# Four subtractions of a key minimum on GpSimd in place of VectorE, in a linear-attention block on one core

## The chip, the cores and the metric

The kernel runs on one core of one Trainium2 chip. The metric is the device time of one execution in microseconds (us). The core has five engines that run their own lists of instructions in order and wait for one another through semaphores: TensorE (PE, matrix products), VectorE (DVE), ScalarE (ACT), GpSimd (POOL) and SyncE (SP, which issues the DMAs here).

## What is computed

One transformer block with adaptive layer norm, a linear attention whose feature map is a pair of softmaxes, and a ReLU network. Batch 1, 2048 rows, width 576, 32 heads of 18, inner width 4608, all bf16.

```python
mod = (silu(c) @ w_mod).reshape(1, 6, 1, 576)          # sa, ca, ga, sb, cb, gb
h = layernorm(x) * (1 + ca) + sa
q, k, v = heads(h @ wqkv)                              # 32 heads of 18
pq, pk = q @ w_phi[head], k @ w_phi[head]
phi_q = concat([softmax(pq), softmax(-pq)])            # 36 features
phi_k = concat([softmax(pk), softmax(-pk)])
kv = sum_s phi_k[s, f] * v[s, d];  z = sum_s phi_k[s, f]
o = (phi_q @ kv) / (phi_q @ z + 1e-6)
x = x + ga * (o @ wo)
h = layernorm(x) * (1 + cb) + sb
x = x + gb * (relu(h @ w1) @ w2)
```

Both softmaxes are made stable by a shift: the first exponentiates pk - max(pk), the second min(pk) - pk, where maximum and minimum run over the 18 features of a head.

## The kernel before

The 2048 rows are 16 tiles of 128 rows. Keys are kept in four blocks of four tiles (`phik`), queries in blocks of two tiles (`room`). A tile has 11 groups of three heads; a group has 108 columns, of which the first 54 hold the key features from the projection, and later the first softmax, and the last 54 the second.

For a pair of key tiles p (p from 0 to 7, two pairs to a block) the softmax goes through these steps, which have short names in the kernel's list:

- KE: ACT copies the projected keys from PSUM into the first 54 columns (helper at L92).
- MN and MX, once for a block: a tree of minima or maxima on DVE (L457, L459, L460), whose last step (L462) writes a `root`. Roots take turns in four buffers.
- LO.p: minimum less key, from the first 54 columns into the last 54 (L470), one instruction over 128 partitions x 1188 elements.
- HI.p: key less maximum, in place in the first 54 columns (L472). It overwrites what LO.p reads, so it comes behind it.
- EX.p: one exponential on ACT over both halves, 2376 elements (L499).
- SU.p and SA.p: the sums, on PE into PSUM (L506) and on DVE (L510), or for two pairs on DVE alone with SD (L517).
- RC.p: the reciprocal, on ACT (L522, L524).
- SC.p: the scaling by it, on DVE (L530).

The queries have the same steps, with a q ahead of the name (qMN, qMX, qLO, qHI, qSA, qSC); their scaling is L534, and they aren't touched by the change. The steps J are the projections on PE (L574, L580), VE and QE copy values and queries out of PSUM on ACT (L92), MH modulates the normalized rows on ACT (L409) or DVE (L410), RW makes the gate rows on PE (L387).

When all keys of a range of tiles are scaled, KVa (tiles 0 to 11), KVb (12 and 13) and KVc (14 and 15) multiply keys and values on PE (L644), 11 products to a tile. KVE copies the result out, NU multiplies it with the first queries (L685), and the network of the first rows follows. A loop over the other seven blocks of 256 rows comes after it, in which PE does the network (L834, L826, L877) while the other engines prepare the next block.

The order of the work in the first stage is written out by hand: a list of step names, run through by a loop that calls each step. The order on PE, DVE, ACT and SP is that of the calls; POOL, too, runs its instructions in the order in which they are issued. Waits are put in by the framework from the tiles that a step reads and writes. Pair p's steps are in block p // 2, at tile p % 2 * 2. A number behind a step's name can choose the engine through the tuple `VA`.

POOL does memsets alone: constants, zero columns of `wk_raw`, `wo_sb`, `phik` and `room` (L203 to L207, L549, L550, L606, L621), and the identity.

Of the kernel before, what the change touches and what calls it, by code (L numbers as in the profile page):

```python
# [13 lines left out]
ALU = mybir.AluOpType  # L14
# [35 lines left out]
def kernel(  # L50
# [23 lines left out]
    V, A_, G, T_ = nc.vector, nc.scalar, nc.gpsimd, nc.tensor  # L74
# [372 lines left out]
    def softmax_parts(E, src, n, whole):  # L447

        ng = n * NG

        def slots(a, s=0):
            return a[:, :, :, s * GF:(s + 1) * GF].rearrange("p n g (f c) -> p (n g) f c", c=G2)

        def ext(op):
            src_, w = src.rearrange("p n g c -> p (n g) c"), 4 * G2
            a = work.tile([P, 4 * NG, w], BF16, name="tree", tag="tree", bufs=1)[:, 0:ng]
            V.tensor_tensor(out=a, in0=src_[:, :, 0:w], in1=src_[:, :, w:2 * w], op=op)  # L457
            for w in (2 * G2, G2):
                V.tensor_tensor(out=a[:, :, 0:w], in0=a[:, :, 0:w], in1=a[:, :, w:2 * w], op=op)  # L459
            V.tensor_tensor(out=a[:, :, 0:G2], in0=a[:, :, 0:G2], in1=src_[:, :, 8 * G2:9 * G2], op=op)  # L460
            r = work.tile([P, 4 * NG, 2, GH], BF16, name="root", tag="root", bufs=4)[:, 0:ng]
            V.tensor_tensor(out=r, in0=a[:, :, 0:GH].unsqueeze(2).to_broadcast([P, ng, 2, GH]),  # L462
                            in1=a[:, :, GH:G2].unsqueeze(2).to_broadcast([P, ng, 2, GH]), op=op)
            return r.rearrange("p a e h -> p a (e h)")

        def less(j, mn, mx):
            f = slots(src[:, j:j + 2])
            r = (mn if mx is None else mx)[:, j * NG:(j + 2) * NG].unsqueeze(2).to_broadcast([P, 2 * NG, DH // 2, G2])
            if mx is None:
                V.tensor_tensor(out=slots(E[:, j:j + 2], 1), in0=r, in1=f, op=ALU.subtract)  # L470
            else:
                V.tensor_tensor(out=slots(E[:, j:j + 2], 0), in0=f, in1=r, op=ALU.subtract)  # L472

        t = {}

        def low_root():
            t["mn"] = ext(ALU.min)

        def low_less(j):
            less(j, t["mn"], None)  # L480

        def high_root():
            t["mx"] = ext(ALU.max)

        def high_less(j):
            less(j, None, t["mx"])

        def low():
            low_root()
            for j in range(0, n, 2):  # L490
                low_less(j)

        def high():
            high_root()
            for j in range(0, n, 2):
                high_less(j)

        def exps(j, k=1):
            A_.activation(out=E[:, j:j + k], in_=E[:, j:j + k], func=ACT.Exp)  # L499

        def sums_pe(j):

            ps = t["s", j] = aux_tile("ps_sum")[:, 0:2 * NG * 2 * G2].rearrange("p (a c) -> p a c", c=G2)
            e = E[:, j:j + 2].rearrange("p n g (s c) -> p (n g) s c", s=2)
            for f in range(DH // 2):
                T_.matmul(ps, lhsT=ident[:], rhs=e[:, :, :, f * G2:(f + 1) * G2], start=(f == 0), stop=(f == DH // 2 - 1))  # L506

        def sums_add(j):
            l = t["l", j] = work.tile([P, 4 * NG, GH], FP32, name="ln_s", tag="ln_s", bufs=2)
            V.tensor_reduce(out=l[:], in_=t["s", j].rearrange("p a (e h) -> p a h e", h=GH), op=ALU.add,  # L510
                            axis=mybir.AxisListType.X)

        def sums(j):
            b, k = j // 2 * 2, j % 2
            if ("l", b) not in t:
                t["l", b] = work.tile([P, 4 * NG, GH], FP32, name="ln_s", tag="ln_s", bufs=2)
            V.tensor_reduce(out=t["l", b][:, k * 22:(k + 1) * 22].rearrange("p (g s) h -> p g s h", s=2), op=ALU.add,  # L517
                            axis=mybir.AxisListType.X, in_=E[:, j].rearrange("p g (s f h) -> p g s h f", s=2, h=GH))

        def recip(j):  # L520
            l = t["l", j]
            A_.activation(out=l[:], in_=l[:], func=ACT.Ln)  # L522
            r = t["r", j] = work.tile([P, 4 * NG, 2, GH], BF16, name="rsum", tag="rsum", bufs=3)
            A_.activation(out=r[:], in_=l[:].unsqueeze(2).to_broadcast([P, 4 * NG, 2, GH]), func=ACT.Exp, scale=-1.0)  # L524

        def scale(j):
            r = t["r", j][:].rearrange("p a e h -> p a (e h)")
            if whole:
                e = E[:, j:j + 2].rearrange("p n g (s f c) -> p (n g s) f c", s=2, c=G2)
                V.tensor_tensor(out=e, in0=e, in1=r.unsqueeze(2).to_broadcast([P, 4 * NG, DH // 2, G2]), op=ALU.mult)  # L530
                return
            for s in range(2):
                e, q = slots(E[:, j:j + 2], s), r.rearrange("p (a s) c -> p a s c", s=2)[:, :, s]
                V.tensor_tensor(out=e, in0=e, in1=q.unsqueeze(2).to_broadcast([P, 2 * NG, DH // 2, G2]), op=ALU.mult)  # L534

        class parts:
            pass
        for f in (low_root, low_less, high_root, high_less, low, high, exps, sums_pe, sums_add, sums, recip, scale):
            setattr(parts, f.__name__, staticmethod(f))
        return parts  # L540
# [214 lines left out]
    soft = {}  # L755
# [36 lines left out]
    p1_ctx = ExitStack()  # L792
    w1 = {}
    ln2 = norm_stats(0, U, xn1[0])
    VA = (V, A_)

    def kvs(t0, t1):
        return lambda: kv_part(t0, t1)
# [92 lines left out]
    def y(n, j, cols=HALVES):  # L891
# [6 lines left out]
    steps = {  # L898
        "RS": lambda u: ln[u][2](), "LX": lambda t, a=0: ln[t // U][4](t % U, VA[a]), "LS": lambda t: ln[t // U][1](t % U), "LT": ln1_T,
        "PT": ln1_pe, "PX": lambda u, c, a=0: ln1_out(u, c, VA[a]), "MH": lambda b, c, a=0: ln1_mod(b, c, VA[a]),  # L900
        "SIL": silu, "WBD": feature_maps, "CR": lambda: V.tensor_copy(out=crep[:], in_=siluc[:].to_broadcast([P, KC, 32])),
        "WT": fold_T, "WTE": lambda g, a=0: fold_T_out(g, VA[a]),
        "F1": lambda c: fold(1, c), "FA1": lambda c, a=0: fold_out(1, c, 0, VA[a]),
        "FB1": lambda c, a=0: fold_out(1, c, 1, VA[a]),
# [5 lines left out]
        "OPEN": open_p1, "PM": pad_keys, "LH": load_maps, "SD": lambda t: soft["K", t // TPB].sums(t % TPB),  # L910
        "J": project, "KE": keys_out, "VE": values_out, "QE": queries_out,
        "MN": lambda b: soft["K", b].low_root(), "MX": lambda b: soft["K", b].high_root(),
        "LO": lambda p: soft["K", p // 2].low_less(p % 2 * 2), "HI": lambda p: soft["K", p // 2].high_less(p % 2 * 2),
        "EX": lambda p: soft["K", p // 2].exps(p % 2 * 2, 2), "SU": lambda p: soft["K", p // 2].sums_pe(p % 2 * 2),
        "SA": lambda p: soft["K", p // 2].sums_add(p % 2 * 2),
        "RC": lambda p: soft["K", p // 2].recip(p % 2 * 2), "SC": lambda p: soft["K", p // 2].scale(p % 2 * 2),
# [27 lines left out]
    MN.0 RS.7 FB0.4 F0.1 KE.7 LT.9 F0.2 LT.11 FA0.4.1 FA0.1.1 FA0.2.1 LT.8 F0.0 FA0.0.1 FB0.1 FB0.0.1 F0.3 FB0.2  # L944
    LS.13 FA0.3.1 J.4.5 RS.6 LO.0 LX.12 KE.4 FB0.3.1 J.34.35 LX.14.1 LX.15 KE.5 LX.13 LT.10 MX.0 MH.2.3.1
    MH.2.0.1 MH.2.1 LM.1 MN.1 QE.2 QE.3 MH.2.4.1 MH.2.2.1 J.32.33 QE.0 LO.1 HI.0 QE.1 J.10.11 KE.10 EX.0 KE.11
    HI.1 LT.15 LT.14 MC2.0 LT.12 LO.3 J.8.9 MX.1 KE.8 LT.13 J.26.27 MH.3.2.1 MH.3.3.1 MH.3.4 LO.2 qMN.0 HI.2
    KE.9 VE.10 MH.3.0.1 LM.2 MH.3.1.1 LM.0 MC2.1 MC2.3 MC2.4 VE.11 MN.2 MC2.2 RW RWE.1 qMX.0 qHI.0 HI.3 MCE2
    EX.2 J.12.13 KE.12 KE.13 LO.4 J.14.15 KE.14 SD.0 SD.1 J.20.21 EX.3 MX.2 KE.15 SU.3 SA.3 EX.1 VE.4 RC.0 VE.5
    SU.2 RD.2 qLO.0 J.22.23 VE.6 qEX.1 qEX.0 J.30.31 SA.2 HI.4 RC.3 VE.14 VE.15 VE.7 LO.5 HI.5 qSU.0 RD.1 MX.3  # L950
    MN.3 qSA.0 EX.4 SU.1 RC.2 J.24.25 VE.8 SU.4 W1 SC.0 J.28.29 qRC.0 LW.0.0 RD.0 VE.9 EX.5 VE.12 SC.2 SA.1 LO.7
    SA.4 SC.3 VE.13 RC.1 J.40.41 QE.8 SU.5 RC.4 J.44.45 HI.7 LO.6 LW.1.1 HI.6 qSC.0 SA.5 EX.6 QE.9 SC.1 QE.12
    J.42.43 EX.7 SC.4 RC.5 QE.13 QE.10 SD.12 SD.13 SC.5 SU.7 SA.7 RC.6 RC.7 KVa SC.6 WOL KVb SC.7 KVc QE.11 WS.1
    qT.0 KVE.1.1 KVE.0 NU.0 NUE.0 NU.1 J.38.39 QE.6 OT.0 OTE.0 NUE.1 OT.1 OTE.1 WS.0 qMX.1 qHI.1 QE.7 WO.0 WOE.0
    WO.1 WOE.1 LW.2.1 J.36.37 QE.4 J.46.47 S2.0 S2.1 R2 QE.14 X2 PN QE.5 PNE P2 qMN.1 LW.0.1 LW.3.0 LW.1.0 QE.15
    LW.3.1 LW.2.0 G.0 FW.2 FW.1 qLO.1 RL.0 qEX.2 qEX.3 qMN.2 qLO.2 qSD.2 RL.2 RL.1 W2.2.0 G.1 qSD.3 W2.1.0 qRC.1
    FW.4 RL.3 W2.0.0 FW.5 W2.0.1 W2.1.1 qMX.2 qHI.2 RL.4 qSC.1 qT.1 W2.2.1 qEX.5 RL.5 G.2 FW.8 RL.6 NV.0 NVE.0
    OU.0 FW.7 NV.1 Y.1.0.0 Y.1.0.1 NVE.1 qEX.4 RL.8 RL.7 Y.1.0.2 OU.1 qSD.4 qSD.5 WP.0 YE.1.0 Y.0.0.0 WPE.0
    qRC.2 qSC.2 S3.0 WP.1 qT.2 WPE.1 Y.0.0.1 Y.0.0.2 S3.1 R3 Y.0.1.0 YE.0.0 Y.1.1.0 Y.0.1.1 X3 XT Y.0.1.2 MD.1
    MD.2 MD.0 MD.4 Y.1.1.1 Y.1.1.2 YE.1.1 MD.3 YE.0.1  # L960
    """
    for step in order.split():
        name, *at = step.split(".")
# [101 lines left out]
```

## Time and profile before

| what | value |
|---|---|
| median of 3 runs | 417.21 us (416.49 to 418.16) |
| profiled execution: time, span | 416.92 us, 415.1 us |
| granted TensorE clock | 0.991 |
| instructions in the span | 9221 |
| PE busy | 402.5 us (97%) |
| DVE busy | 235.3 us (57%) |
| ACT busy | 180.9 us (44%) |
| POOL busy | 7.7 us (2%) |

The span runs from the first to the last instruction of the profiled execution; the rest of its time lies around it. Busy time counts instructions of an engine, not how fast they run. In a row of the timeline stand the start, the time from there to the end, engine, line, operation, output and input, sizes, and how many instructions are merged; in brackets the idle time before it and what ended it. In a row of groups stand busy time and mean duration in ns, and behind the bar the idle time before. L470 is line 470 of the kernel.

### The profile page before, as it was taken

The page shows a single profiled execution, that of the slowest core. Times are in us where ns is not written, and L with a number is a line of the kernel's source. Part 1 is how long each engine was busy: PE and PEld are TensorE (multiplying, and loading weights), DVE is VectorE, ACT ScalarE, POOL GpSimd, SP SyncE. Part 2 cuts the span into 40 slices and gives each one's busy share as a digit, 9 for nine tenths or more (in the row PEclk, how much of TensorE's full clock was granted, in tenths as well). Part 3 has the DMA queues.
Part 4 walks back from the last instruction along what each step waited for, and adds up shares of the span by engine and source line. Part 5 has one row for each costly group of instructions (what it writes and reads, how often), then busy time and mean ns, then how long its engine had stood idle before and what let it go on. Part 6 is the DMA issues. An engine that isn't in the chain of part 4 may idle for free.

```text
span 415.1 us, 9221 instructions
## 1 busy us (share of the span) xinstructions
PE 402.5 (97%) x3966; PEld 321.8 (78%) x3967; DVE 235.3 (57%) x602; ACT 180.9 (44%) x294; POOL 7.7 (2%) x27
## 2 busy tenths in 40 slices
PE   5999999989999999999999999999999999999997
PEld 4666667676888888788878887888888788878876
DVE  8798999987948464637345552846192533330011
ACT  5699999944761064006302630452055014302400
POOL 5100000000000000000000000000000000000000
PEclk9699999999999999999999999999999999999999
DMA  8969670489774220501051214203210601010001
GB/s 267 265 117 199 176 189 9 50 249 365 247 168 81 55 48 2 117 14 33 12 106 31 17 33 85 47 0 69 63 34 0 117 20 30 16 32 16 2 0 30
DMA packets 70906, 35.43 MB, mean 85 GB/s; under 512 B 55373, under 2 KB 68498, under 8 KB 70866
## 3 DMA queue, kind: packets, MB, share of 16 engines
q1 hardware_dynamic: 70264, 34.82, 35.5%
q8 instruction: 31, 0.51, 0.5%
q10 hardware_dynamic: 602, 0.02, 0.1%
q14 instruction: 9, 0.07, 0.1%
HBM read 19.26 MB, written 2.36 MB: 52 GB/s over the span
## 4 chain that ended last, share of the span: by engine, by line
PE 86%; DMA 5%; ACT 5%; DVE 2%; issue 1%; SPq 0%; ACTq 0%
PE ps_y L877 34%; PE ps_h L834 31%; PE ps_h L826 4%; PE ps_q L574 3%; PE ps_wo L742 3%; PE ps_v L574 2%; DMA hT<-xn 2%; PE ps_sum L506 2%; DMA wma<-in_w_mod_dram 2%; PE ps_wo L440 2%; ACT hT L409 1%; PE ps_kv L644 1%; PE ps_k L574 1%; ACT phik L92 1%; DMA wk_raw<-in_A_wqkv_dram 1%; PE ps_num L685 1%
## 5 line engine op out<-in xcount | busy, mean ns | idle before, releaser
L839 ACT ACTIVATE H<-ps_h 128x1024 bf16<-128x1024 f32 x72 | 73.6, 1023 | 172.1 <-PE ps_h L826 123.7
L877 PE MATMUL ps_y<-w_sb,H 128*128 128x288 bf16 (+2 forms) x1188 | 142.8, 282 | 0.0
L877 PEld LDWEIGHTS <-H 128*128 128x128 bf16 x1188 | 113.7, 98 | 27.3
L834 PE MATMUL ps_h<-hT,w1a 128*128 128x256 bf16 x640 | 74.9, 273 | 0.3 <-DVE hT L410 0.3
L834 PEld LDWEIGHTS <-w1a 128*128 128x128 bf16 x640 | 61.2, 98 | 9.9 <-issue 2.7
L885 DVE TENSOR_TENSOR outt<-ps_y,row_gb 128x288 bf16<-128x288 f32 (+2 forms) x33 | 14.8, 448 | 89.0 <-PE ps_y L877 89.0
L834 PE MATMUL ps_h<-hT,w1b 128*128 128x256 bf16 x512 | 59.0, 273 | 0.0
L834 PEld LDWEIGHTS <-w1b 128*128 128x128 bf16 x512 | 49.8, 98 | 6.5 <-issue 0.6
L574 PEld LDWEIGHTS <-hT 128*128 128x128 bf16 x384 | 35.3, 98 | 15.1 <-issue 5.2
L747 DVE TENSOR_TENSOR x_sb<-x_sb,ps_wo 128x288 bf16<-128x288 bf16 x28 | 12.6, 451 | 31.4 <-PE ps_wo L742 24.8
L228 DVE BATCH_NORM_STATS2 bst<-x_sb 128x6 f32<-128x288 bf16 x64 | 25.6, 442 | 0.1
L826 PE MATMUL ps_h<-hT,w1c 64*128 64x256 bf16 x288 | 19.9, 271 | 0.0
L574 PE MATMUL ps_k<-wfold,hT 128*128 128x270 bf16 (+1 forms) x128 | 19.2, 292 | 0.1
L499 ACT ACTIVATE room<-room 128x1188 bf16<-128x1188 bf16 x16 | 18.8, 1187 | 0.5
L517 DVE TENSOR_REDUCE ln_s<-room 128x66 f32<-128x1188 bf16 x14 | 18.9, 1365 | 0.0
L574 PE MATMUL ps_v<-wv_sb,hT 128*128 128x288 bf16 x128 | 18.2, 287 | 0.0
L574 PE MATMUL ps_q<-wfold,hT 128*128 128x270 bf16 (+1 forms) x128 | 17.9, 286 | 0.0
L499 ACT ACTIVATE phik<-phik 128x2376 bf16<-128x2376 bf16 x8 | 17.6, 2198 | 0.0
L237 DVE TENSOR_SCALAR xn<-x_sb,mv,rstd 128x576 bf16<-128x576 bf16 x16 | 6.1, 426 | 20.1 <-ACT rstd L233 20.1
L826 PEld LDWEIGHTS <-w1c 64*128 64x128 bf16 x288 | 12.1, 94 | 5.2 <-issue 3.8
L459 DVE TENSOR_TENSOR tree<-tree 128x264 bf16<-128x264 bf16 (+2 forms) x48 | 14.6, 304 | 1.7
L410 DVE TENSOR_SCALAR hT<-hT,mod 128x256 bf16<-128x256 bf16 (+1 forms) x40 | 11.5, 349 | 6.1 <-DMA hT<-xn 6.1
(133 smaller groups left out, 363.6 us busy)
## 6 DMA issues: line engine op xcount, KB each, us to landing
w_sb<-in_B_w_dram SPq DMA_DIRECT2D x6, 864.0 KB, 11.6
out_dram<-outt SPq DMA_DIRECT2D x15, 144.0 KB, 2.3
w1b<-in_B_w_dram SPq DMA_DIRECT2D x2, 1024.0 KB, 7.3
x_sb<-in_A_x_dram SPq DMA_DIRECT2D x3, 576.0 KB, 6.0
w1a<-in_B_w_dram SPq DMA_DIRECT2D x2, 768.0 KB, 6.9
wma<-in_w_mod_dram SPq DMA_DIRECT2D x2, 576.0 KB, 6.5
wmb<-in_w_mod_dram SPq DMA_DIRECT2D x1, 1152.0 KB, 6.1
wmb<-in_w_mod_dram SPq DMA_DIRECT2D x2, 576.0 KB, 5.4
```

Source lines behind the costliest of these rows:

```text
L228: V.bn_stats(out=st[:, half, :], in_=x_sb[:, t0 + j, half * 288:(half + 1) * 288])
L459: V.tensor_tensor(out=a[:, :, 0:w], in0=a[:, :, 0:w], in1=a[:, :, w:2 * w], op=op)
L499: A_.activation(out=E[:, j:j + k], in_=E[:, j:j + k], func=ACT.Exp)
L517: V.tensor_reduce(out=t["l", b][:, k * 22:(k + 1) * 22].rearrange("p (g s) h -> p g s h", s=2), op=ALU.add, axis=mybir.AxisListType.X, in_ ...
L574: T_.matmul(ps[:, i, 0:cn], lhsT=lhs[:, ci, :], rhs=w[:, ci, cs:cs + cn], start=(first and ci == 0), stop=(not first and ci == 4))
L742: T_.matmul(p[:, 0:cn], lhsT=oTs[n, j][:, ci, :], rhs=wo_sb[:, ci, cs:cs + cn], start=False, stop=(ci == 3))
L747: V.tensor_tensor(out=xs[:, cs:cs + cn], in0=xs[:, cs:cs + cn], in1=p[:, 0:cn], op=ALU.add)
L826: T_.matmul(f1[q][:, e, hh * w:hh * w + w], lhsT=w1["c"][r, 2 * q + hh, :], rhs=hT[r, 4, :], start=(first and hh == 0), stop=(not first an ...
L834: T_.matmul(f1[q][:, e, hh * w:hh * w + w], lhsT=w1_at(2 * q + hh, e, ci), rhs=hT[:, ci, :], start=(first and hh == 0 and ci == 0), stop=( ...
L839: A_.activation(out=p2t["H1"].rearrange("p (e j) n -> p e j n", e=2)[:, :, 2 * q:2 * q + 2], in_=f1[q][:].rearrange("p e (h n) -> p e h n" ...
L877: T_.matmul(ps[:, 0, 0:cn], lhsT=p2t["H1"][:, k, j * P:(j + 1) * P], rhs=p2t["w2"][:, k, c], start=(k == 0), stop=(k == NJ - 1))
L885: V.tensor_tensor(out=o[:, c], in0=ps[:, 0, 0:cn], in1=rows["gb"][:, c], op=ALU.mult)
```

## The change

In four of the eight pairs (3, 5, 7 and 6) the step LO is issued on GpSimd instead of VectorE. The step list keeps its order; `VA` has GpSimd as its third entry, and LO takes a number that chooses from it. In the compiled lists DVE has four instructions of L470 fewer, POOL has them behind its memsets, and PE, ACT and SP have the same lists as before. New waits: the four instructions on POOL wait for DVE's root and ACT's key copies; on DVE, the last step of qMX.0's tree (its root's buffer held the minimum that LO.3 reads), HI.5, HI.7 and HI.6 wait for POOL.

```diff
-        def less(j, mn, mx):
+        def less(j, mn, mx, e=V):
             f = slots(src[:, j:j + 2])
             r = (mn if mx is None else mx)[:, j * NG:(j + 2) * NG].unsqueeze(2).to_broadcast([P, 2 * NG, DH // 2, G2])
             if mx is None:
-                V.tensor_tensor(out=slots(E[:, j:j + 2], 1), in0=r, in1=f, op=ALU.subtract)
+                e.tensor_tensor(out=slots(E[:, j:j + 2], 1), in0=r, in1=f, op=ALU.subtract)
             else:
-                V.tensor_tensor(out=slots(E[:, j:j + 2], 0), in0=f, in1=r, op=ALU.subtract)
+                e.tensor_tensor(out=slots(E[:, j:j + 2], 0), in0=f, in1=r, op=ALU.subtract)
...
-        def low_less(j):
-            less(j, t["mn"], None)
+        def low_less(j, e=V):
+            less(j, t["mn"], None, e)
...
-    VA = (V, A_)
+    VA = (V, A_, G)
...
-        "LO": lambda p: soft["K", p // 2].low_less(p % 2 * 2), "HI": lambda p: soft["K", p // 2].high_less(p % 2 * 2),
+        "LO": lambda p, a=0: soft["K", p // 2].low_less(p % 2 * 2, VA[a]), "HI": lambda p, a=0: soft["K", p // 2].high_less(p % 2 * 2, VA[a]),
...
-    HI.1 LT.15 LT.14 MC2.0 LT.12 LO.3 J.8.9 MX.1 KE.8 LT.13 J.26.27 MH.3.2.1 MH.3.3.1 MH.3.4 LO.2 qMN.0 HI.2
+    HI.1 LT.15 LT.14 MC2.0 LT.12 LO.3.2 J.8.9 MX.1 KE.8 LT.13 J.26.27 MH.3.2.1 MH.3.3.1 MH.3.4 LO.2 qMN.0 HI.2
...
-    SU.2 RD.2 qLO.0 J.22.23 VE.6 qEX.1 qEX.0 J.30.31 SA.2 HI.4 RC.3 VE.14 VE.15 VE.7 LO.5 HI.5 qSU.0 RD.1 MX.3
+    SU.2 RD.2 qLO.0 J.22.23 VE.6 qEX.1 qEX.0 J.30.31 SA.2 HI.4 RC.3 VE.14 VE.15 VE.7 LO.5.2 HI.5 qSU.0 RD.1 MX.3
...
-    MN.3 qSA.0 EX.4 SU.1 RC.2 J.24.25 VE.8 SU.4 W1 SC.0 J.28.29 qRC.0 LW.0.0 RD.0 VE.9 EX.5 VE.12 SC.2 SA.1 LO.7
-    SA.4 SC.3 VE.13 RC.1 J.40.41 QE.8 SU.5 RC.4 J.44.45 HI.7 LO.6 LW.1.1 HI.6 qSC.0 SA.5 EX.6 QE.9 SC.1 QE.12
+    MN.3 qSA.0 EX.4 SU.1 RC.2 J.24.25 VE.8 SU.4 W1 SC.0 J.28.29 qRC.0 LW.0.0 RD.0 VE.9 EX.5 VE.12 SC.2 SA.1
+    LO.7.2 SA.4 SC.3 VE.13 RC.1 J.40.41 QE.8 SU.5 RC.4 J.44.45 HI.7 LO.6.2 LW.1.1 HI.6 qSC.0 SA.5 EX.6 QE.9 SC.1
```

More of the change, by code (lines that the diff above doesn't have):

```diff
@@ L477, in low_root, with high_less @@
             t["mn"] = ext(ALU.min)
-        def low_less(j):
-            less(j, t["mn"], None)
+        def low_less(j, e=V):
+            less(j, t["mn"], None, e)
         def high_root():
             t["mx"] = ext(ALU.max)
-        def high_less(j):
-            less(j, None, t["mx"])
+        def high_less(j, e=V):
+            less(j, None, t["mx"], e)
         def low():
@@ L951 @@
-    MN.3 qSA.0 EX.4 SU.1 RC.2 J.24.25 VE.8 SU.4 W1 SC.0 J.28.29 qRC.0 LW.0.0 RD.0 VE.9 EX.5 VE.12 SC.2 SA.1 LO.7
-    SA.4 SC.3 VE.13 RC.1 J.40.41 QE.8 SU.5 RC.4 J.44.45 HI.7 LO.6 LW.1.1 HI.6 qSC.0 SA.5 EX.6 QE.9 SC.1 QE.12
-    J.42.43 EX.7 SC.4 RC.5 QE.13 QE.10 SD.12 SD.13 SC.5 SU.7 SA.7 RC.6 RC.7 KVa SC.6 WOL KVb SC.7 KVc QE.11 WS.1
-    qT.0 KVE.1.1 KVE.0 NU.0 NUE.0 NU.1 J.38.39 QE.6 OT.0 OTE.0 NUE.1 OT.1 OTE.1 WS.0 qMX.1 qHI.1 QE.7 WO.0 WOE.0
-    WO.1 WOE.1 LW.2.1 J.36.37 QE.4 J.46.47 S2.0 S2.1 R2 QE.14 X2 PN QE.5 PNE P2 qMN.1 LW.0.1 LW.3.0 LW.1.0 QE.15
@@ L956 @@
[L956 to L960, printed above, removed]
+    SU.2 RD.2 qLO.0 J.22.23 VE.6 qEX.1 qEX.0 J.30.31 SA.2 HI.4 RC.3 VE.14 VE.15 VE.7 LO.5.2 HI.5 qSU.0 RD.1 MX.3
@@ new lines @@
+    MN.3 qSA.0 EX.4 SU.1 RC.2 J.24.25 VE.8 SU.4 W1 SC.0 J.28.29 qRC.0 LW.0.0 RD.0 VE.9 EX.5 VE.12 SC.2 SA.1
+    LO.7.2 SA.4 SC.3 VE.13 RC.1 J.40.41 QE.8 SU.5 RC.4 J.44.45 HI.7 LO.6.2 LW.1.1 HI.6 qSC.0 SA.5 EX.6 QE.9 SC.1
+    QE.12 J.42.43 EX.7 SC.4 RC.5 QE.13 QE.10 SD.12 SD.13 SC.5 SU.7 SA.7 RC.6 RC.7 KVa SC.6 WOL KVb SC.7 KVc
+    QE.11 WS.1 qT.0 KVE.1.1 KVE.0 NU.0 NUE.0 NU.1 J.38.39 QE.6 OT.0 OTE.0 NUE.1 OT.1 OTE.1 WS.0 qMX.1 qHI.1 QE.7
+    WO.0 WOE.0 WO.1 WOE.1 LW.2.1 J.36.37 QE.4 J.46.47 S2.0 S2.1 R2 QE.14 X2 PN QE.5 PNE P2 qMN.1 LW.0.1 LW.3.0
@@ new lines @@
+    LW.1.0 QE.15 LW.3.1 LW.2.0 G.0 FW.2 FW.1 qLO.1 RL.0 qEX.2 qEX.3 qMN.2 qLO.2 qSD.2 RL.2 RL.1 W2.2.0 G.1 qSD.3
+    W2.1.0 qRC.1 FW.4 RL.3 W2.0.0 FW.5 W2.0.1 W2.1.1 qMX.2 qHI.2 RL.4 qSC.1 qT.1 W2.2.1 qEX.5 RL.5 G.2 FW.8 RL.6
+    NV.0 NVE.0 OU.0 FW.7 NV.1 Y.1.0.0 Y.1.0.1 NVE.1 qEX.4 RL.8 RL.7 Y.1.0.2 OU.1 qSD.4 qSD.5 WP.0 YE.1.0 Y.0.0.0
+    WPE.0 qRC.2 qSC.2 S3.0 WP.1 qT.2 WPE.1 Y.0.0.1 Y.0.0.2 S3.1 R3 Y.0.1.0 YE.0.0 Y.1.1.0 Y.0.1.1 X3 XT Y.0.1.2
+    MD.1 MD.2 MD.0 MD.4 Y.1.1.1 Y.1.1.2 YE.1.1 MD.3 YE.0.1
```

## The prediction

> **What bounds the kernel now.** I read the page first (engine totals and the chain that ended last), then busy time by stage, then the timelines of VectorE, ScalarE, GpSimd and TensorE around the four moved steps.
>
> ```profile
> PE 402.5 (97%) x3966; PEld 321.8 (78%) x3967; DVE 235.3 (57%) x602; ACT 180.9 (44%) x294; POOL 7.7 (2%) x27
> PE 86%; DMA 5%; ACT 5%; DVE 2%; issue 1%; SPq 0%; ACTq 0%
> ```
>
> Over the whole span TensorE (PE) is the bound, VectorE (DVE) is busy for little more than half, and GpSimd (POOL) does nothing after its memsets. That average invites the change and hides where it takes place: all four steps lie between 41 and 80 us.
>
> ```profile
> core 0: us, PE busy (x) PEld busy (x) DVE busy (x) ACT busy (x) POOL busy (x), PEclk, DMA share, GB/s
> 36.00:50.40 14.40, 13.63 (x152) 9.32 (x151) 13.78 (x33) 14.40 (x30) 0.00 (x0) 1.00 1.02 229
> 50.40:84.00 33.60, 33.59 (x290) 22.85 (x291) 32.35 (x55) 32.98 (x54) 0.00 (x0) 1.00 0.41 85
> 106.00:415.00 309.00, 306.12 (x2904) 252.73 (x2900) 142.10 (x377) 96.33 (x114) 0.00 (x0) 1.00 0.23 49
> ```
>
> In the stages of the keys three engines are full at once. From 36 to 50 us ScalarE (ACT) is busy throughout, from 50 to 84 us PE for 33.59 of 33.60 us, and DVE lacks only 0.62 and 1.25 us, a good part of it the 30 ns between dependent instructions. DVE time that is freed here meets a full PE, and DVE time that is added has almost no idle time to vanish in. After 106 us everything hangs on PE, so what is lost by then is not regained.
>
> **What is removed.** Four subtractions (LO.3, LO.5, LO.7, LO.6), each one instruction of 128x1188, leave DVE's list. Their rows, with what stands around them:
>
> ```profile
> 40.67 0.34 DVE L462 TENSOR_TENSOR root<-tree 128x264 bf16<-128x264 bf16 x1
> 40.93 0.77 DVE L470 TENSOR_TENSOR phik<-root,phik 128x1188 bf16<-128x1188 bf16 x1
> 41.62 1.46 DVE L472 TENSOR_TENSOR phik<-phik,root 128x1188 bf16<-128x1188 bf16 x2
> 42.99 0.77 DVE L470 TENSOR_TENSOR phik<-root,phik 128x1188 bf16<-128x1188 bf16 x1
> 42.96 2.28 ACT L499 ACTIVATE phik<-phik 128x2376 bf16<-128x2376 bf16 x1
> 43.68 0.70 DVE L457 TENSOR_TENSOR tree<-phik 128x1056 bf16<-128x1056 bf16 x1
> 50.90 0.34 DVE L462 TENSOR_TENSOR root<-tree 128x264 bf16<-128x264 bf16 x1
> 52.61 0.25 DVE L462 TENSOR_TENSOR root<-tree 128x132 bf16<-128x132 bf16 x1
> 55.60 2.68 DVE L517 TENSOR_REDUCE ln_s<-phik 128x66 f32<-128x1188 bf16 x2
> 62.72 0.77 DVE L470 TENSOR_TENSOR phik<-root,phik 128x1188 bf16<-128x1188 bf16 x1
> 63.52 0.78 DVE L472 TENSOR_TENSOR phik<-phik,root 128x1188 bf16<-128x1188 bf16 x1
> 68.38 0.34 DVE L462 TENSOR_TENSOR root<-tree 128x264 bf16<-128x264 bf16 x1
> 68.64 0.42 DVE L510 TENSOR_REDUCE ln_s<-ps_sum 128x132 f32<-128x264 f32 x1
> 68.99 2.69 DVE L530 TENSOR_TENSOR phik<-phik,rsum 128x2376 bf16<-128x2376 bf16 x2
> 71.94 0.77 DVE L470 TENSOR_TENSOR phik<-root,phik 128x1188 bf16<-128x1188 bf16 x1
> 72.62 0.42 DVE L510 TENSOR_REDUCE ln_s<-ps_sum 128x132 f32<-128x264 f32 x1
> 74.27 0.77 DVE L472 TENSOR_TENSOR phik<-phik,root 128x1188 bf16<-128x1188 bf16 x1
> 74.96 0.77 DVE L470 TENSOR_TENSOR phik<-root,phik 128x1188 bf16<-128x1188 bf16 x1
> 75.76 0.78 DVE L472 TENSOR_TENSOR phik<-phik,root 128x1188 bf16<-128x1188 bf16 x1
> ```
>
> LO.3 is the row at 42.99, LO.5 at 62.72, LO.7 at 71.94, LO.6 at 74.96. Instructions overlap a little, so the price is the distance to the next start: 43.68 - 42.99 = 0.69, 0.80, 0.68 and 0.80 us, 2.97 us together. No other engine's list changes, and no DMA moves past anything.
>
> **What is added on POOL.** No row shows POOL doing this operation, so its duration T is bounded from its other rows:
>
> ```profile
> L206 POOL MEMSET v<- 128x128 bf16 x4 | 2.3, 883 | 0.1
> L621 POOL MEMSET room<- 128x440 bf16 x2 | 0.9, 466 | 18.2 <-PE ps_fold L373 18.2
> L606 POOL MEMSET room<- 128x216 bf16 x3 | 0.7, 274 | 0.0
> masks.py:199 POOL TENSOR_SCALAR_AFFINE_SELECT ident<-ident 128x128 bf16<-128x128 bf16 x1 | 0.3, 293 | 0.0
> masks.py:197 POOL MEMSET ident<- 128x128 bf16 x1 | 0.2, 207 | 0.3 <-POOLq L1049 0.3
> ```
>
> Writing costs (466 - 274) / (440 - 216) = 0.86 ns an element above a fixed 0.09 us (274 ns - 216 x 0.86). The select, which reads 128 elements as well as writing them, took 293 - 207 = 86 ns more than the memset of the same size: 0.67 ns for an element read. The subtraction writes one stream and reads two: 0.86 + 2 x 0.67 = 2.20 ns, times 1188, plus 0.09, is T = 2.7 us, an estimate. The lower end is the write alone, 0.09 + 1188 x 0.86 ns = 1.1 us; the upper is the pace of the memset of scattered elements, 2.3 us / 4 / 128 = 4.5 ns an element, 5.3 us. I take 2.7, since it counts streams by dense rows and the subtraction runs over dense rows of 54.
>
> **When it runs, and who waits.** POOL has nothing else queued, so each subtraction is free to start when its minimum stands: LO.3 at 41.01 (the root at 40.67), LO.5 at 51.24 (the root at 50.90), over eleven us ahead of its old place, LO.7 and LO.6 back to back from 68.72. Three waits on POOL come in on DVE: the root of qMX.0 (52.61), which reuses the buffer of the minimum that LO.3 reads; HI.5; and HI.7 with HI.6, which overwrite in place what LO reads. Behind each is all of DVE's list and, through EX, ACT. With T = 2.7 and nothing disturbed, these waits cost nothing: the root has nine us to spare, HI.5 more, and HI.6, which would come at 75.76 - 2.97 = 72.8, finds LO.6 done at 68.72 - 1.49 + 5.4 = 72.6. So the waits don't decide; what the engines do to one another does.
>
> **The shared port.** Twice the trace catches POOL beside DVE:
>
> ```profile
> 4.27 0.88 POOL L207 MEMSET wo_sb<- 128x576 bf16 x1
> 4.64 0.54 DVE L315 TENSOR_SCALAR sg<-sg 128x5 f32<-128x5 f32 x1
> 13.17 0.79 DVE L250 TENSOR_SCALAR xn<-x_sb,mv,rstd 128x640 bf16<-128x640 bf16 x2
> 13.29 0.38 POOL L550 MEMSET phik<- 128x20 bf16 x1
> 15.11 0.12 POOL L550 MEMSET phik<- 128x20 bf16 x1
> 54.53 0.17 DVE L353 TENSOR_SCALAR mod<-mod 128x5 f32<-128x5 f32 x1
> 5.44 0.17 DVE L317 TENSOR_TENSOR siluc<-ccol,sg 128x5 bf16<-128x5 f32 x1
> ```
>
> A tensor_scalar of five elements took 0.54 us beside POOL's memset and ended where that ended (5.18 and 5.15 us); an equal one took 0.17 with POOL idle. The other way, a memset of 20 columns took 0.38 us while DVE ran the tensor_scalar over 640, and 0.12 with DVE idle. So one engine holds the other up until its instruction is over, in both directions. But the tensor_tensor at 5.44, with two inputs in SBUF, took its normal 0.17 us while POOL's memsets went on, and neither case has POOL reading two tensors. What the traces bear out is that the two exclude each other in some pairings; the pairing that the change makes is not shown.
>
> The Trainium skill, in "SBUF — State Buffer", section "SBUF: two separate sides", names the pairings: a VectorE instruction in a two-port mode, or one with two SBUF inputs against a GpSimd instruction that reads SBUF, takes the shared ports for its whole length, and the later one fully blocks. By that rule the 5.44 row was free because a memset reads nothing, and the change makes just the pairing that blocks; the sum would be the one that follows.
>
> **The sum, with full exclusion.** Nearly all of DVE's list here is tensor_tensor from SBUF. Where POOL has its turn, DVE stands for T, less what it does from PSUM meanwhile.
> - LO.3: asks at 41.0, starts when the row at 40.93 ends (41.70). DVE loses 2.70 and saves 0.69: +2.0. At once this passes to ACT: the exponential EX.0 needs HI.0, started at 42.96 with HI.0 (41.62 + 0.77) ready 0.57 us before, and ACT is full until 50.4.
> - LO.5: falls on the tree of qMX.0 at some 51 us: 2.70 - 0.80 = +1.9.
> - LO.7 and LO.6: from 68.7 on, 5.4 us. Beside them only qSA.0 (0.35 us, from PSUM) runs; SC.0 at 68.99 stands. 5.4 - 0.68 - 0.80 - 0.35 = +3.6.
>
> Together 7.5 us. Who needs DVE last are the products of keys and values:
>
> ```profile
> 85.21 2.69 DVE L530 TENSOR_TENSOR phik<-phik,rsum 128x2376 bf16<-128x2376 bf16 x2
> 83.80 5.23 PE L644 MATMUL ps_kv<-v,phik 128*128 128x57 bf16 x176
> 90.77 0.78 PE L685 MATMUL ps_num<-KVZ,ET 108*128 108x57 bf16 x22 [1.75 <-DVE KVZ L658]
> ```
>
> The last scale ends at 87.90; the first product that reads it is number 155 of 176, at 83.80 + 154 x 5.23 / 176 = 88.38. So 0.48 us is slack and 7.0 us reaches the end, as PE's order is fixed and nothing behind 89 us goes ahead without these products. The profiled execution took 416.92 us (span 415.1, 1.8 around it; the median of the runs is 417.21): 416.92 + 7.0 = 423.9 us. With T at 1.1 the sum is 4 x 1.1 - 2.97 - 0.35 - 0.48 = +0.6 (417.5 us), at 5.3 it is +17.4 (434.3 us).
>
> **Rivals.**
> - **DVE keeps the port, POOL comes late (chance 0.17).** DVE's instructions follow within 30 ns, so a waiting POOL might get in only where DVE stops. LO.3 then runs while the root of qMX.0 waits for it (+2.70 - 0.69); LO.5 beside the two reductions at 55.60, which read one tensor (-0.80); LO.7 and LO.6 while HI.7 and HI.6 wait (5.4 - 1.48 = +3.9). Sum 5.1 - 0.48 = +4.6: 421.5 us. For it: DVE's dense list. Against it: dependent instructions leave gaps, in which a request that is already standing should win.
> - **Both run side by side (0.21), the case that is not slower.** Its place is any tensor_tensor of DVE during LO.3; if those keep their 0.70 to 0.77 us, the port doesn't block this pairing. DVE is then 2.97 us ahead, and nothing takes it up: PE had 0.01 us idle from 50.4 to 84, ACT 0.62. Price: between -0.6 and 0, 416.9 us. It holds up to T = 2.8 us, from where HI.6 waits for LO.6; the wait eats the lead until T is some 4 us, and only then costs time. For it stands the row at 5.44.
> - **POOL is much slower than its dense rows (0.08).** The patterns repeat rows of six elements; at 4.5 ns an element and full exclusion the time is 434 us.
> - **A gain over 0.5% (0.04).** It needs PE or ACT to be waiting for DVE in this stretch; the stage rows show no such idle time, so this is for what I have not seen.
> - **The change doing something other than it says** is no case: the compiled lists show the four instructions on POOL, gone from DVE, all else in place.
>
> **How the numbers follow.** Full exclusion near T = 2.7 has the remaining 0.50: 423.9 us, alone from 421 to 427.5 (T from 2.0 to 3.6). Forecast 424 us. Range 416.7 to 428: it takes in both cases below, and leaves out the slow POOL and the gain. What a measurement of this kernel can tell from no change is about 0.5%, 2.1 us. Slower by more: 0.50 + 0.17 + 0.08 = 0.75. Within: 0.21. Faster: 0.04.
>
> **What would show it.** In the changed profile: POOL rows of L470 near 2.7 us; a tensor_tensor of DVE stretched by some 2 us near 42, 54 and twice after 70; EX.0 about 2 us late; idle time of PE before the sums or the products, waiting for ACT or DVE. I am wrong if DVE's rows keep their length beside POOL's, if T is under 1.5 us, or if PE is still full from 50 us to the products at 84.

## The result and the profile after

The changed kernel takes 421.42 us (median of 4 runs, 420.43 to 423.44), the kernel before 417.43 in the same comparison: a ratio of 1.0103 (95% interval 1.0060 to 1.0146), slower by some 4 us. Measured again with more rounds it is 1.0118 (1.0087 to 1.0149), slower by 4.9 us, between 3.6 and 6.2. The forecast was +7.0 us.

The page of the changed kernel, its engine totals, and its stages as shown of before:

```profile
PE 405.5 (96%) x3966; PEld 322.8 (77%) x3967; DVE 240.3 (57%) x598; ACT 181.2 (43%) x294; POOL 18.3 (4%) x31
36.00:50.40 14.40, 13.29 (x117) 8.62 (x115) 13.95 (x30) 12.73 (x29) 3.27 (x3) 1.00 1.03 234
50.40:84.00 33.60, 31.44 (x298) 21.39 (x298) 32.46 (x53) 29.59 (x49) 8.10 (x3) 1.00 0.25 67
```

Four instructions have left DVE, and its busy time has grown from 235.3 to 240.3 us. Between 50 and 84 us PE now has 2.2 idle microseconds and ACT 4.0, where before they had 0.01 and 0.6. (This execution is already 2.07 us late at its first tree behind 36 us, which starts at 38.38 and not at 36.31, ahead of anything the change touches. The two windows therefore don't hold quite the same work, and times below are taken as distances within an execution.)

GpSimd's rows and those of DVE beside them, from the timelines of the changed kernel:

```profile
43.26 2.64 POOL L470 TENSOR_TENSOR phik<-root,phik 128x1188 bf16<-128x1188 bf16 x1 [6.63 <-DVE root L462]
54.85 2.45 POOL L470 TENSOR_TENSOR phik<-root,phik 128x1188 bf16<-128x1188 bf16 x1 [8.95 <-ACT row_four L92]
73.24 5.65 POOL L470 TENSOR_TENSOR phik<-root,phik 128x1188 bf16<-128x1188 bf16 x2 [15.94 <-DVE root L462]
43.00 0.77 DVE L470 TENSOR_TENSOR phik<-root,phik 128x1188 bf16<-128x1188 bf16 x1
43.68 3.54 DVE L472 TENSOR_TENSOR phik<-phik,root 128x1188 bf16<-128x1188 bf16 x2
54.74 0.43 DVE L457 TENSOR_TENSOR tree<-pq 128x528 bf16<-128x528 bf16 x1
55.21 2.52 DVE L459 TENSOR_TENSOR tree<-tree 128x264 bf16<-128x264 bf16 x2
73.02 0.42 DVE L510 TENSOR_REDUCE ln_s<-ps_sum 128x132 f32<-128x264 f32 x1
73.36 6.78 DVE L530 TENSOR_TENSOR phik<-phik,rsum 128x2376 bf16<-128x2376 bf16 x2
```

Each subtraction of GpSimd lies on a stretched row of DVE: the pair HI.0 and HI.1 takes 3.54 us (1.46 before), two steps of the tree of qMX.0 2.52 us (0.57 before), the scalings SC.0 and SC.2 6.78 us (2.69 before). That is 2.08 + 1.95 + 4.09 = 8.12 us more for 2.97 us saved. The instruction of DVE that had begun when GpSimd asked (43.00, 54.74) kept its length; the next one stood. A tree step of some 0.3 us and a scaling of 1.39 us lose the same 2 us, so DVE stands still and isn't merely slowed. In the last pair the two engines took turns, as the durations of one line show (minimum, median, maximum in ns):

```profile
L530 DVE TENSOR_TENSOR phik<-phik,rsum x2: 3403/3429/3455, 73.4 to 76.7; 128x2376 bf16<-128x2376 bf16 x2
L470 POOL TENSOR_TENSOR phik<-root,phik x4: 2266/2547/3417, 43.3 to 75.5; 128x1188 bf16<-128x1188 bf16 x4
```

Both scalings are 2.0 us longer than their 1.386, and one subtraction is 3.4 us long, as it waited its turn behind a scaling. So the row of a GpSimd instruction holds its own wait as well; the shortest of the four, 2.27 us, began beside a reduction from PSUM and waited for nothing. What followed, in ACT's timeline and PE's:

```profile
46.57 2.18 ACT L499 ACTIVATE phik<-phik 128x2376 bf16<-128x2376 bf16 x1 [1.32 <-DVE phik L472]
60.00 2.18 ACT L499 ACTIVATE phik<-phik 128x2376 bf16<-128x2376 bf16 x1 [1.39 <-DVE mod L352]
62.23 2.54 PE L506 MATMUL ps_sum<-phik,ident 128*128 128x264 bf16 x18 [0.94 <-ACT phik L499]
90.31 5.23 PE L644 MATMUL ps_kv<-v,phik 128*128 128x57 bf16 x176
```

ACT, which had no idle time ahead of EX.0 and EX.3 before, waits 1.3 and 1.4 us for DVE there; PE then waits for ACT. The products of keys and values begin 90.31 - 38.38 = 51.93 us behind the first tree after 36 us; before it was 83.80 - 36.31 = 47.49. This stage is 4.44 us longer. No wait of DVE for GpSimd stands in the list of waits.

### The profile page after: what moved, and what is told of

The parts are those of the page before. It is cut to its first block, busy times and chain, and to the rows that moved or that the text cites. A ratio compares the mean times of both kernels' runs of the same rounds, so it can differ in the third digit from the quotient of the medians.

```text
span 421.7 us, 9227 instructions
## 1 busy us (share of the span) xinstructions
PE 405.5 (96%) x3966; PEld 322.8 (77%) x3967; DVE 240.3 (57%) x598; ACT 181.2 (43%) x294; POOL 18.3 (4%) x31
## 4 chain that ended last, share of the span: by engine, by line
PE 79%; DVE 11%; ACT 4%; DMA 3%; issue 1%; SPq 0%; DVEq 0%; ACTq 0%
PE ps_y L877 33%; PE ps_h L834 30%; PE ps_h L826 4%; PE ps_wo L742 3%; DVE tree L459 2%; DMA wma<-in_w_mod_dram 2%; PE ps_wo L440 2%; DVE phik L530 2%; DVE phik L472 2%; DVE tree L457 1%; PE ps_q L574 1%; PE ps_kv L644 1%; ACT phik L499 1%; PE ps_k L574 1%; DMA wk_raw<-in_A_wqkv_dram 1%
## 5 line engine op out<-in xcount | busy, mean ns | idle before, releaser
L574 PE MATMUL ps_k<-wfold,hT 128*128 128x270 bf16 (+1 forms) x128 | 20.7, 305 | 0.2
L574 PE MATMUL ps_v<-wv_sb,hT 128*128 128x288 bf16 x128 | 19.1, 295 | 1.1 <-ACT phik L92 1.1
L499 ACT ACTIVATE room<-room 128x1188 bf16<-128x1188 bf16 x16 | 18.8, 1188 | 0.5
L459 DVE TENSOR_TENSOR tree<-tree 128x264 bf16<-128x264 bf16 (+2 forms) x48 | 16.6, 345 | 1.7
```

Source lines behind the costliest of these rows:

```text
L574: T_.matmul(ps[:, i, 0:cn], lhsT=lhs[:, ci, :], rhs=w[:, ci, cs:cs + cn], start=(first and ci == 0), stop=(not first and ci == 4))
```

## The experiments

Two quantities are read from one profiled execution of each kernel. One is the time by which DVE's rows are stretched. The other is the stage: from the tree of MX.0 (the row of L457 at 36.31 before), which lies ahead of all moved steps, to the first product of keys and values. The stage is free of what happens in the loading at the start. It is still one execution: the kernel with memsets, in which DVE does the same work in the same time as before, has a stage 0.47 us shorter, so differences of that size say nothing.

| kernel | GpSimd's new work | DVE stretched, us | stage, us | ratio to before (95%) |
|---|---|---|---|---|
| before | none | | 47.49 | 1 |
| changed, again | four subtractions, taken from DVE | 8.1 | 51.95 | 1.0118 (1.0087 to 1.0149) |
| twice | four subtractions, DVE keeps its own | 8.1 | 55.11 | 1.0200 (1.0169 to 1.0231) |
| reads | four copies, one stream read | 3.7 | 51.84 | 1.0113 (1.0087 to 1.0138) |
| writes | eight memsets | 0 | 47.02 | 1.0031 (1.0008 to 1.0055) |
| copies | none, DVE's LO made shorter | | 47.15 | 1.0020 (0.9996 to 1.0044) |
| only LO.5 | one subtraction, in tensor_tensor work | 2.0 | 47.90 | 1.0015 (0.9993 to 1.0036) |
| LO.5 under cover | one subtraction, beside reductions | 0 | 47.27 | 0.9987 (0.9967 to 1.0008) |
| only LO.7 and LO.6 | two subtractions | 4.1 | 49.37 | 1.0086 (1.0052 to 1.0120) |

**The changed kernel again**, for its interval.

> The changed kernel once more, beside the runs below. Exclusion theory (VectorE's tensor_tensor stands still while GpSimd's subtraction holds a shared port, about 2.05 us each by the stretched rows of the changed kernel's trace): four times 2.05 less the 2.97 us of instructions taken away and 0.48 us of slack is +4.7 us, some 421.5 to 422. Side-by-side theory (nothing is held up, the lost time comes from the new waits on GpSimd or from a disturbed execution): within 0.5% of before once it is measured in more rounds.

The time is 422.14 us where 416.59 stands for before, and its trace has the same stretched rows (3.53, 2.52 and 6.79 us). The loss is there in both measurements and both traces; side by side is out.

**What a microsecond of DVE is worth here.** One line of the kernel before:

```diff
-                V.tensor_tensor(out=slots(E[:, j:j + 2], 1), in0=r, in1=f, op=ALU.subtract)
+                (V.tensor_copy(out=E[:, j:j + 2, :, GF:], in_=src[:, j:j + 2]) if whole else V.tensor_tensor(...))
```

> All eight minimum subtractions of the keys are left out: VectorE copies the keys in their place (a one-source copy instead of a tensor_tensor, about 0.33 us shorter each, 2.6 us together, close to the 2.97 us that the change takes from VectorE). GpSimd does nothing new. My step: freed VectorE time meets a full TensorE and ScalarE, so the time moves by 0 to -0.6 us, 416.5 to 417.4. Rival, VectorE is on the path here and each microsecond taken from it shortens the kernel: -2.1 to -2.6 us, 414.8 to 415.3.

The groups of DVE in this kernel show the saving, and PE's timeline what comes of it:

```profile
L470 DVE COPY phik<-phik 128x1188 bf16<-128x1188 bf16 x7 | 3.2, 464 | 0.0
83.56 5.23 PE L644 MATMUL ps_kv<-v,phik 128*128 128x57 bf16 x176
```

The eight are 0.30 us shorter each (464 for 769 ns). Seven of them lie in the stage, 2.1 us, and the stage becomes 0.34 us shorter, which is within what two executions differ by; the time doesn't fall. So DVE time that is freed in the kernel before is worth next to nothing, and the 2.97 us that the change saves were no gain before any price of GpSimd's is counted.

**The price without the saving.**

```diff
+            G.tensor_tensor(out=slots(spare), in0=r, in1=slots(src[:, j:j + 2]), op=ALU.subtract)
...
+        soft["K", p // 2].spare_less(p % 2 * 2, pq[1][:, 0:2])
+        soft["K", p // 2].low_less(p % 2 * 2)
```

> GpSimd does the four subtractions of the change, at the same place and with the same waits, into a spare place in the query tile; VectorE keeps all its own as before. Exclusion theory: four holds of 2.05 us without the 2.97 us saved, less 0.48 slack, +7.7 us, 425.1, and four stretched tensor_tensor rows. Side by side: no row stretched and no change, 417.4. If the loss of the changed kernel comes from the waits of VectorE on GpSimd, about the same +4 us as there, without stretched rows.

```profile
40.87 2.64 POOL L484 TENSOR_TENSOR room<-root,phik 128x1188 bf16<-128x1188 bf16 x1 [6.63 <-DVE root L462]
41.29 3.53 DVE L472 TENSOR_TENSOR phik<-phik,root 128x1188 bf16<-128x1188 bf16 x2
53.51 2.52 DVE L459 TENSOR_TENSOR tree<-tree 128x264 bf16<-128x264 bf16 x2
72.54 6.81 DVE L534 TENSOR_TENSOR phik<-phik,rsum 128x2376 bf16<-128x2376 bf16 x2
```

In this timeline (L484 is the added subtraction, L534 the scaling) the same three rows are stretched by 2.07, 1.95 and 4.12 us. The stage grows by 7.62 us and the time by 2.0%, 8.3 us. The loss is DVE standing still; taking the instructions off DVE gives 55.11 - 51.95 = 3.16 us of it back. Once the others wait for DVE, the saving counts in full, which it didn't in the kernel with copies.

**Writing alone.** In place of that subtraction:

```diff
+            G.tensor_copy(out=flat[:, 0:6], in_=t["mn"][:, j * NG, :])
+            for _ in range(2):
+                G.memset(flat, 0.0)
```

> VectorE keeps all its own as before; at the four places GpSimd reads six elements of the minimum (so that it starts where the subtraction did) and then runs two memsets of 128x1188, some 2.2 us that write and read nothing. If any GpSimd instruction over SBUF holds up VectorE's tensor_tensor: four holds of about 2.2 us, +8 us, 425. If only one that reads does (the rule of the Trainium skill, SBUF - State Buffer, section SBUF: two separate sides): four tiny holds of 0.1 to 0.2 us, 417.4 to 418.2, no stretched tensor_tensor rows during the memsets.

```profile
41.51 2.23 POOL L486 MEMSET room<- 128x1188 bf16 x2
41.32 1.46 DVE L472 TENSOR_TENSOR phik<-phik,root 128x1188 bf16<-128x1188 bf16 x2
68.60 2.23 POOL L486 MEMSET room<- 128x1188 bf16 x2
68.48 2.69 DVE L536 TENSOR_TENSOR phik<-phik,rsum 128x2376 bf16<-128x2376 bf16 x2
```

GpSimd is as busy as with the subtraction, beside the very rows that it stretched, and these keep 1.46 and 2.69 us; the stage is not longer. To hold up a tensor_tensor, a GpSimd instruction has to read. The timed ratio lies a little above 1 (by 0.08 to 0.55%), which no row of its trace shows. Some 0.2 us of it lies outside the span (time less span is 1.98 us on average, 1.80 before); the rest stays open.

**Reading one stream.** Against the kernel with memsets, the large instruction is a copy:

```diff
-            for _ in range(2):
-                G.memset(flat, 0.0)
+            G.tensor_copy(out=slots(spare), in_=slots(src[:, j:j + 2]))
```

> VectorE keeps all its own; GpSimd copies at the four places the 128x1188 keys that the subtraction would read into the spare place (one read stream and one write stream, no second input), started by six elements of the minimum. If the holding needs GpSimd to read SBUF and no more: four stretched tensor_tensor rows, each by the time of the copy's streams, 1.0 to 2.0 us, so +3.5 to +7.5 us, 420 to 424. If it needs two inputs on GpSimd's side: no stretched rows and 416.6 to 417.5, as with the memsets.

```profile
43.14 1.61 POOL L485 COPY room<-phik 128x1188 bf16<-128x1188 bf16 x1
42.95 2.44 DVE L472 TENSOR_TENSOR phik<-phik,root 128x1188 bf16<-128x1188 bf16 x2
54.07 1.42 DVE L459 TENSOR_TENSOR tree<-tree 128x264 bf16<-128x264 bf16 x2
71.98 3.67 DVE L535 TENSOR_TENSOR phik<-phik,rsum 128x2376 bf16<-128x2376 bf16 x2
75.92 1.65 DVE L470 TENSOR_TENSOR phik<-root,phik 128x1188 bf16<-128x1188 bf16 x1
71.85 0.19 POOL L484 COPY room<-root 128x6 bf16<-128x6 bf16 x1 [16.45 <-DVE root L462]
74.46 1.24 POOL L484 COPY room<-root 128x6 bf16<-128x6 bf16 x1
85.89 2.10 PE L579 MATMUL ps_q<-wfold,hT 128*128 128x270 bf16 x8
87.78 1.86 PE L511 MATMUL ps_sum<-phik,ident 128*128 128x264 bf16 x9
```

One input is enough: stretched by 0.98, 0.85, 0.98 and 0.88 us (L535 is the scaling, L485 the copy). A copy holds DVE for some 0.9 us, the subtraction with its two streams for 2.05. GpSimd waits in the same way: its copy of six elements (L484) takes 0.19 us when nothing is ahead of it and 1.24 us behind a scaling. The time grows by 1.13%, 4.7 us (3.6 to 5.8), within what was expected. The stage grows by 4.35 us, more than the 3.69 by which DVE's rows are stretched. The last two rows say why: ahead of the products TensorE ran these 17 matmuls in 2.10 and 1.86 us, where rows of the same kind take 1.15 and 1.35, and its mean granted clock from 85.5 to 89.5 us was 0.57. In the kernel twice it was 1.00 at the same place. So up to 1.46 us of this stage is the clock and not the hold; whether it fell in the other executions isn't shown.

**The same subtraction beside other work of DVE.** LO.5 alone, where the change puts it, and LO.5 held back to the two reductions SD.0 and SD.1:

```diff
-    EX.2 J.12.13 KE.12 KE.13 LO.4 J.14.15
+    EX.2 J.12.13 KE.12 KE.13 LO.4 GL.5 J.14.15
...
-    VE.7 LO.5.2 HI.5
+    VE.7 HI.5
...
+        "GL": lambda p: (G.tensor_copy(out=phik_g(2)[:, 2, 0, GF:GF + 6], in_=phik_g(2)[:, 1, NG - 1, DW - 6:DW]), soft["K", p // 2].low_less(p % 2 * 2, G)),
```

> LO.5 alone on GpSimd, LO.3, LO.7 and LO.6 back on VectorE. Exclusion: one hold of 2.05 us in the tree of qMX.0, 0.80 saved, 0.48 slack: +0.8 us, 417.4 on a before of 416.6. Side by side: 0.

> LO.5 alone on GpSimd, but held back (by a copy of six elements that reads the end of LO.4) until VectorE begins its two tensor_reduce of 2.68 us together, which read one tensor from SBUF. If the exclusion concerns VectorE instructions with two SBUF inputs (or a two-port mode): both reductions keep 1.38 us each, at most 0.3 us of the tree behind them is held up, and the time is that of before, 0 +- 0.6 us, with VectorE up to 0.8 us ahead. If GpSimd's reading shuts VectorE out of SBUF whatever it does: a reduction of about 3.4 us, and +0.8 us as with LO.5 alone.

First the timeline of LO.5 alone, then that with the cover:

```profile
51.38 2.43 POOL L470 TENSOR_TENSOR phik<-root,phik 128x1188 bf16<-128x1188 bf16 x1 [16.88 <-DVE root L462]
51.70 2.53 DVE L459 TENSOR_TENSOR tree<-tree 128x264 bf16<-128x264 bf16 x2
```

```profile
56.81 2.27 POOL L470 TENSOR_TENSOR phik<-root,phik 128x1188 bf16<-128x1188 bf16 x1
56.39 2.68 DVE L517 TENSOR_REDUCE ln_s<-phik 128x66 f32<-128x1188 bf16 x2
58.99 0.70 DVE L457 TENSOR_TENSOR tree<-phik 128x1056 bf16<-128x1056 bf16 x1
```

Beside reductions, which read one tensor from SBUF, nothing is stretched: 2.68 us as before, and the tree behind keeps 0.70. GpSimd's row, waiting for nobody, is 2.27 us. In time the two can't be told apart (their intervals overlap, and both hold 1): LO.5 alone costs between -0.3 and 1.5 us, which takes in both the 0.8 expected and nothing at all, and the covered one between -1.4 and 0.3. The stages, 47.90 and 47.27 us, differ the way the rows say, but by little more than two executions do; the rows carry this comparison. So what shuts DVE out here is the pairing, a tensor_tensor with two inputs in SBUF against a GpSimd instruction that reads. That is the rule of the Trainium skill, "SBUF — State Buffer", section "SBUF: two separate sides"; the three cases of this study (memset 0, copy some 0.9, reduction 0 us of stretch) bear it out. They don't separate the number of inputs from the kind of DVE's operation, since the reduction was the only operation with a single SBUF tensor that was set beside such an instruction. Nor is every other operation free: by the prediction's row at 4.64, a tensor_scalar took 0.54 us beside a mere memset and 0.17 without it.

**Half of the change.** LO.7 and LO.6 on GpSimd, the others back:

```diff
-    HI.1 LT.15 LT.14 MC2.0 LT.12 LO.3.2 J.8.9
+    HI.1 LT.15 LT.14 MC2.0 LT.12 LO.3 J.8.9
...
-    VE.7 LO.5.2 HI.5
+    VE.7 LO.5 HI.5
```

> LO.7 and LO.6 alone on GpSimd, the other two back on VectorE. Exclusion: two holds, two scalings of about 3.4 us in place of 1.38 each (+4.1), 1.48 saved, 0.48 slack: +2.1 us, 418.7. GpSimd and VectorE take turns, so HI.7 and HI.6 don't wait. If the loss of the changed kernel lies in its first two steps, which delay the exponentials EX.0 and EX.3: no change here.

```profile
68.32 5.65 POOL L470 TENSOR_TENSOR phik<-root,phik 128x1188 bf16<-128x1188 bf16 x2 [34.05 <-DVE root L462]
68.41 6.82 DVE L530 TENSOR_TENSOR phik<-phik,rsum 128x2376 bf16<-128x2376 bf16 x2
85.39 5.23 PE L644 MATMUL ps_kv<-v,phik 128*128 128x57 bf16 x176
```

The scalings stand for 4.13 us, and the stage grows by 1.88 (2.1 expected). The timed 0.86% is 3.6 us, its interval (2.2 to 5.0) starting just above the expectation. The profiled execution was the shortest of the seven (418.51 us), so its stage doesn't show all of that. The seven had a mean granted clock of 0.988, the 24 of before 0.990; how much of the difference this makes stays open. The part of the change that delays neither EX.0 nor EX.3 costs as well: the loss is paid by the subtraction, not by where ACT is hit first.

No version came out ahead of the kernel before; the covered one is level with it.

## Why the prediction was right, and where it was too high

**The bound.** Three full engines from 41 to 84 us, so that DVE's freed time is worth 0 to 0.6 us: shown by the copies (2.1 us freed in the stage, which moved by 0.34 us; the time didn't fall).

**The mechanism.** Full exclusion, the likeliest case: shown by the stretched rows, and by the twice kernel, which pays without the saving. Side by side is out by the same rows.

**The size of one hold.** This is the term that was mis-sized. The sum let DVE stand for T, GpSimd's whole row, at 2.7 us; DVE stood only 1.95 to 2.08 us a subtraction. Four times 0.65 us is 2.6 us, nearly all that lies between the forecast +7.0 and the stage's +4.44. With 2.05 in place of 2.7 the prediction's own sum gives +4.4; that it comes so near is helped by two smaller errors, told below, which nearly cancel (0.35 us credited in vain, 0.7 us absorbed for 0.48). Two things are in the 0.65. T itself was too long: the subtraction that waits for nobody takes 2.27 us, 0.43 less. The price of writing was right (1.1 us for 1188 elements, the memset's 2.23 / 2), while the 0.67 ns for an element read, taken from a single select over 128 elements, comes out as (2.27 - 1.115) us / 2 / 1188 = 0.49 ns. The other 0.2 us is the step from a row to a hold: in the changed kernel GpSimd's first row ends at 45.90, while DVE's two subtractions of 1.46 us, which end at 47.22, must have gone on at 45.76. That the mean of GpSimd's four rows is 2.69 us, just T, is luck: they hold GpSimd's own waits.

**The likeness to a rival.** The rival in which POOL comes late forecast 421.5 us, and 421.42 was measured, nearer than the forecast of 424. That agreement is chance, and the time alone wouldn't have told the two apart; the rows do. LO.5 ran in the tree of qMX.0 at 54.85 and not beside the reductions, and none of DVE's waits in the list is for GpSimd. The range of 416.7 to 428 took in three of the cases, so that a time within it says little.

**The third item of the sum.** The 0.35 us credited for qSA.0 beside LO.7 did not show: the two scalings lost 4.09 us, two whole holds. The turns between the engines, which the sum did not work out, neither added nor saved anything.

**The slack and the path.** 8.12 - 2.97 = 5.15 us of DVE came out as 4.44 at the products: 0.7 us was absorbed where 0.48 had been counted, and in another place. The sum let the last scaling carry the loss to the products. The rows show it going through ACT; first those of before, then those of the changed kernel:

```profile
76.81 2.17 ACT L499 ACTIVATE phik<-phik 128x2376 bf16<-128x2376 bf16 x1
80.05 2.20 ACT L499 ACTIVATE phik<-phik 128x2376 bf16<-128x2376 bf16 x1
82.61 1.35 PE L506 MATMUL ps_sum<-phik,ident 128*128 128x264 bf16 x9
```

```profile
83.54 2.18 ACT L499 ACTIVATE phik<-phik 128x2376 bf16<-128x2376 bf16 x1 [0.65 <-DVE phik L472]
86.79 2.20 ACT L499 ACTIVATE phik<-phik 128x2376 bf16<-128x2376 bf16 x1
89.05 1.35 PE L506 MATMUL ps_sum<-phik,ident 128*128 128x264 bf16 x9
```

Before, EX.6 (76.81) started 0.27 us behind the end of HI.6, and the sums SU.7, just ahead of the products, 0.36 us behind the end of EX.7 (82.25), as PE was full. In the changed kernel EX.6 waits for HI.6, which ends at 83.50, and SU.7 starts as EX.7 ends (88.99). Those two margins, and 0.23 us in which DVE had waited for ACT at 61.68, account for what was absorbed, less the 0.04 and 0.06 us that now lie between an end and the start behind it. At the last scaling 0.20 us of the 0.48 is still left (it ends at 92.00 + 2.69 = 94.69, and product 155 comes at 94.89).

**The late port.** GpSimd was not kept waiting until DVE stops; it came in behind the instruction that was running (43.68, 55.21). The gap between dependent instructions, or the end of one, is enough.

**The waits.** HI.5, HI.7, HI.6 and the root of qMX.0 never waited for GpSimd, as worked out.

**On ACT.** EX.0 starts 46.57 - 38.38 = 8.19 us behind the first tree, before it was 42.96 - 36.31 = 6.65: 1.5 us late where some 2 were expected: the hold of 2.08 less the 0.57 us by which HI.0 had been early.

## What to carry to other kernels

Ask first what the engine to be relieved holds up: an instruction taken from it pays only where another engine waits for it. In this kernel elementwise work that was moved to GpSimd didn't run beside VectorE's tensor_tensor from SBUF; VectorE saved 0.74 us an instruction and stood for 2.05. If such work must go there, hold it back until VectorE runs reductions, the one case that was free here, and look in the trace for rows on either side that are longer than their kind.

## What had not been expected of the hardware

- The hold is shorter than GpSimd's row: 2.05 us where the row shows 2.45 to 2.64, and 2.27 when it waits for nobody. The difference between a row and a hold is GpSimd's own wait and a short stretch at its end, in which DVE already runs.
- A GpSimd read of one stream of 1188 bf16 costs a tensor_tensor of DVE about 0.9 us, one of two streams, in a subtraction, 2.05.
- Under demand from both sides the engines alternate by instruction: two subtractions and two scalings ran in turn, each scaling 2.0 us longer.
